# A fused spectral-mix and GEGLU backward kernel: feed-forward groups begin on eight transposed row tiles, and the transform of x is issued as pieces between the steps

## The chip, the cores and the metric

The kernel runs on one core of a Trainium2 chip. The metric is the device time of one execution in microseconds (us). The kernel before was run three times; the median is 1459.56 us.

A core has five engines with queues of their own, each strictly in the order of the program: TensorE (PE in the profile; PEld are its weight loads), VectorE (DVE), ScalarE (ACT), GpSimd (POOL) and SyncE (SP). SP issues nearly all transfers here; POOL and ACT issue a few.

## The reference, cut to what matters

The forward pass mixes two branches of x (2048 rows of 576, bf16) by a gate for each row, and the kernel returns the output and all seven gradients.

```python
def _A_ref(x, w_r, w_i):
    X = rfft2(x.astype(float32), axes=(-2, -1)) * (w_r + 1j * w_i)
    return irfft2(X, s=(S, D), axes=(-2, -1)).astype(bfloat16)

def _B_ref(x, w_gate, w_up, w_down):
    return (gelu_tanh(x @ w_gate) * (x @ w_up)) @ w_down      # 576 -> 4608 -> 576

g = sigmoid((x * gate_w).sum(-1, keepdims=True))
out = g * _A_ref(x, w_r, w_i) + (1 - g) * _B_ref(x, w_gate, w_up, w_down)
# and the vjp of out for grad_out: x, w_r, w_i, w_gate, w_up, w_down, gate_w
```

## The kernel before, in words

**Names.** Rows lie on 128 partitions as 16 row tiles (T = 16): `xn` holds x, `dB` grad_out ("dO"). Their transposes, which matmuls with the weights and with the tables need, are `xT` and `dOT`. The Fourier transforms are matmuls with cosine and sine tables that the kernel builds at its start: `build_D` (tables along the 576 columns, `Dt`), `build_R` (rotation angles along the rows, four row tiles a call, `Rt`), `columns_B` and `build_B` (`Btab`, for the last 32-point stage). Each ends in a Sin on ACT; those of R and B are put on a list, `tb.late`, and issued when `run_late` or a pop empties it.

**The head (L841 to L876).** SP loads x, grad_out and the gate and up weights of the first group, all rows first. `tchunk` (L335) transposes four row tiles on PE and copies them from PSUM, two copies on DVE and one on ACT. Between the four chunks of x and the four of grad_out stands the whole forward transform of x: for each row tile a first half `u1` (L546; six matmuls with `Dt`, then one copy on ACT to Y) and a second half `u2` (L561; two matmuls with `Rt`, a copy `ve` on ACT, an add and a subtract on DVE to Vt at L574 and L575, a store to DRAM). The down-projection weights of group 0 come in two steps: `load_w(0, 1)` are two transposing loads, `load_w(0, 2)` five copies into `wdT`; `load_w(0, 0)` are six loads into `wgu`. Last stands `gate()` (L355): 80 one-column matmuls, a Sigmoid on ACT and four small operations on DVE, which give `omg32` (1 - g) and `gs32` to all that follows. The head takes its PSUM from three pools in turn (`headps`, L330): pg (one buffer), ph (two) and pz (one).

**The steps (L935 to L1006).** The 4608 hidden columns are 18 groups of 256, and each group has four steps of four row tiles. A step is: `H_mm` (L370), the products z = dOT with wdT (L380, L383) and xy = xT with wgu (L387, L394) in two halves; `H_da` (L401), ACT scales z into da; `H_act` (L407), ACT takes q, xb and hu from each half of xy; `H_ew1` (L416), three operations on DVE; `H_ew2` (L432), two Sigmoids on ACT (om and s, L435 and L436) and eight operations on DVE (L440 to L447), which give A, dHg and dHu. From group 1 on a step also issues pieces of the weight gradients of the group before (`W_units`, L460; matmuls at L480, L497 and L510, copies on ACT at L458), each with a weight in microseconds (1.0 or 1.7).

**The slots.** The other transforms are a list of pieces, `fft` (L882): the forward transform of grad_out (`fg`, 16 first and 16 second halves), the turned tables, the middle (`mid_units`: products with the filter, 74 slots, with their DVE work on a list of its own, `side`) and the two inverse transforms. `fft_next` issues the next piece. How many pieces have to be issued by the end of a step, `want` says (L901): four a step in group 0, then by a weighted share up to step 65. In a step from group 1 on the first piece stands in the middle of the second half of xy, the others among the weight-gradient pieces where the weights passed so far reach 1.0, 3.0 and 5.0 (L982), and what is left over at the step's end. A piece takes its PSUM from `pftile` (L533): in group 0 from pg and pz in turn, later, when pg has been given up, only from pz, which z uses too. `scale_dB` (L930) multiplies half of dB by omg32 on DVE, after step 3 and after step 4.

**The end.** After the steps, from about 1024 us, PE computes b and the gradient of x from A, dHg and dHu, which are loaded back from DRAM (`block`, L1089).

The functions that the change touches, and what calls them:

Of the kernel before, what the change touches and what calls it, by code (L numbers as in the profile page):

```python
# [30 lines left out]
FG = 256  # L31
# [195 lines left out]
def kernel(  # L227
# [40 lines left out]
    def load_w(g, part):  # L268

        fsl = slice(g * FG, (g + 1) * FG)  # L270
        if part == 0:
            wts[g] = (wpool.tile([P, 5, 2 * FG], BF16, tag="wgu", name="wgu"), wpool.tile([P, 5, FG], BF16, tag="wdT", name="wdT"))
# [28 lines left out]
    for k in range(4):  # L301
        load_x(4 * k)
    for k in range(4):
        load_do(4 * k)
    load_w(0, 0)
# [29 lines left out]
    def tchunk(src, dst, t0, copy=None):  # L335
        for k, cs in enumerate(((0, 1), (2, 3), (4,))):
            pool, tag = headps()
            tp_ = pool.tile([P, 2, 2, 4, P], BF16, tag=tag, name="tp")
            for j, c in enumerate(cs):
                for tt in range(4):  # L340
                    if c < 4:
                        nc.tensor.transpose(tp_[:, 0, j, tt, :], src[:, t0 + tt, eo(c)], ident[:])
                    else:
                        for r in (LO, HI):
                            nc.tensor.transpose(tp_[r, 0, 0, tt, :], src[:, t0 + tt, 512:D], ident[:])
            o = dst[:, cs[0]:cs[0] + len(cs), t0:t0 + 4, :]
            i = tp_[:, 0, 0:len(cs)]
            if copy:
                copy(o, i)
            elif k == (t0 // 4) % 2:  # L350
                nc.scalar.copy(o, i)
            else:
                V.tensor_copy(o, i)

    def gate():  # L355
        lps = head_tile()[:, 0]
        for t in range(T):
# [3 lines left out]
        nc.scalar.activation(g_bf[:], lps[:, 0:T], ACT.Sigmoid)  # L361
        V.tensor_copy(g32[:], g_bf[:])
        V.tensor_scalar(omg_bf[:], g32[:], -1.0, 1.0, op0=ALU.mult, op1=ALU.add)
        V.tensor_copy(omg32[:], omg_bf[:])
        V.tensor_scalar(gs32[:], g32[:], SD2, None, op0=ALU.mult)
# [177 lines left out]
    def fwd_units(src, dst, scale, ps=pftile, vevac=None):  # L543
# [17 lines left out]
        def u2(t):  # L561
            def f():
# [278 lines left out]
    def head_tile():  # L841
        pool, tag = headps()
        return pool.tile([P, 2, 512], F32, tag=tag, name="fx")
# [6 lines left out]
    with nc.allow_non_contiguous_dma(reason="tiny gate_w column load"):  # L850
        for par in range(2):
            nc.gpsimd.dma_start(gwT[:, 2 * par:2 * par + 2], gate_w[par:512:2].rearrange("(k p) -> p k", p=P))
        nc.gpsimd.dma_start(gwT[HI, 4:5], gate_w[512:D].rearrange("(p o) -> p o", o=1))
    x1, x2 = fwd_units(xT, scr_x, None, ps=head_tile)
    build_R(nc, tb, unit, 0)
    run_late(tb)
    for t in range(T):
        x1[t]()
        if t in (6, 11):
            load_w(0, 1 + t // 11)  # L860
        if t % 4 == 2 and t < 14:
            tchunk(xn, xT, t + 2)
        if t >= 9 and t % 2 == 1:
            tchunk(dB, dOT, 2 * (t - 9))
        if t % 4 == 1 and t + 3 < T:
            build_R(nc, tb, unit, t + 3)
        if t == 13:
            build_B(nc, tb, unit, res)
        if tb.late:
            tb.late.pop(0)()  # L870
        if t > 1:
            x2[t - 2]()
    run_late(tb)
    x2[T - 2]()
    x2[T - 1]()
    gate()  # L876

    fg = zipped(*fwd_units(dOT, scr_g, gs32))
# [17 lines left out]
    mid_at = 2 * T + 10  # L896
    NPR = NT // 2
    LASTP = NG * NPR - 7
    done = [0]

    def want(pr):  # L901

        n0 = 4 * NPR
        if pr < NPR:
            return 4 * (pr + 1)

        def load(n):

            return n + 0.7 * min(max(n - mid_at, 0), n_mid)
# [25 lines left out]
    for g in range(NG):  # L935
# [3 lines left out]
        for m in range(NPR):  # L939
# [9 lines left out]
            if g == 0 and m > 0:  # L949
                fft_next()  # L950
# [6 lines left out]
            if g == 0:  # L957
                fft_next()
            if pr == 0:
                fft_next()  # L960
# [3 lines left out]
            def second():  # L964
                xy = xy_full(1, fft_next if n or g == 0 else None)
# [3 lines left out]
                side_work(1.4)  # L969

            def sigs():
                H_ew2(g, m, tiles, state[0], da)
                side_work(1.4)
            if g == 0:
                second()
                fft_next()
# [270 lines left out]
```

## Time and profile before

| | us |
|---|---|
| three runs | 1459.56, 1457.01, 1460.73 |
| median | 1459.56 |
| the profiled execution, its own time | 1458.92 |
| its span in the profile | 1457.1 |
| first z matmul (L380), step 0 | 49.84 |
| first z of steps 1, 2 and 3 | 60.10, 72.71, 84.37 |
| first z of step 4 (group 1) and step 5 | 96.03, 110.67 |
| first matmul of the last stage (L1092) | 1023.84 |

The mean granted clock of TensorE is 0.992 of full speed over the span. A row of a profile view names the line, the engine, the operation and the tiles, out <- in; idle time ahead of it stands in brackets with what released it.

### The profile page before, as it was taken

The numbers are of one execution on the slowest core, as the hardware profiler recorded it, in microseconds if no ns is written. First come the engines' busy times: TensorE is split into PE (matmuls) and PEld (weight loads), VectorE is DVE, ScalarE is ACT, GpSimd is POOL, SyncE is SP. The second block draws the span as 40 slices with busy tenths as digits, with TensorE's granted clock in tenths as the row PEclk, the third lists the DMA queues.
The fourth block names the chain that finished last, engine by engine and source line by source line (L and its number), as shares of the span: only waits on it lengthen the run. The fifth ranks groups of instructions, "written<-read, shape, count | busy, mean of one in ns | idle before, by whom it ended". The sixth has DMA issues, their size and how long they took to land.

```text
span 1457.1 us, 28112 instructions
## 1 busy us (share of the span) xinstructions
PE 1386.9 (95%) x11342; PEld 1023.7 (70%) x11414; DVE 731.4 (50%) x1394; ACT 715.5 (49%) x1311; POOL 125.6 (9%) x230
## 2 busy tenths in 40 slices
PE   6888998999999999999999999999999999999997
PEld 4555666676676676677767667668777777777776
DVE  6676456876866776755666565553000652212200
ACT  5776767776677777667766767663000000000000
POOL 3001010000010011001001001000000110000000
PEclk9999999999999999999999999999999999999999
DMA  5333363445645554453554554857999997887773
GB/s 190 94 103 105 92 167 108 135 123 142 166 122 134 146 155 117 113 160 105 151 145 122 144 161 121 182 130 175 242 179 188 234 220 158 170 159 156 163 151 76
DMA packets 516477, 214.96 MB, mean 148 GB/s; under 512 B 312921, under 2 KB 510554, under 8 KB 516346
## 3 DMA queue, kind: packets, MB, share of 16 engines
q1 hardware_dynamic: 506714, 192.65, 56.8%
q0 software_dynamic: 7824, 19.49, 4.3%
q8 instruction: 89, 1.46, 0.4%
q10 hardware_dynamic: 1808, 1.02, 0.2%
q14 instruction: 42, 0.34, 0.1%
HBM read 40.76 MB, written 93.84 MB: 92 GB/s over the span
## 4 chain that ended last, share of the span: by engine, by line
PE 82%; ACT 9%; DVE 3%; issue 3%; SPq 1%; DMA 1%; POOL 0%; ACTq 0%; DVEq 0%; POOLq 0%
PE acc L1092 28%; PE wps L497 16%; PE xy L394 14%; PE z L380 8%; PE wps L480 7%; PE xy L387 2%; PE wps L510 2%; PE z L383 1%; ACT om L435 1%; ACT xb L413 1%; ACT hu L414 1%; ACT q L411 1%; DMA pin<-scr 1%; ACT Xx L666 1%; ACT s L436 1%
## 5 line engine op out<-in xcount | busy, mean ns | idle before, releaser
L1092 PEld LDWEIGHTS <-pin 128*128 128x128 bf16 x3456 | 337.3, 98 | 87.5 <-DMA pin<-scr 1.8
L394 PE MATMUL xy<-wgu,xT 128*128 128x512 bf16 x1080 | 258.8, 380 | 10.1 <-issue 9.4
L497 PEld LDWEIGHTS <-xn 128*128 128x128 bf16 x2304 | 224.4, 98 | 38.2 <-issue 0.2
L394 PEld LDWEIGHTS <-xT 128*128 128x128 bf16 x1152 | 106.5, 98 | 138.2 <-issue 32.3
L404 ACT ACTIVATE da<-z,omg 128x256 bf16<-128x256 f32 x288 | 112.8, 474 | 118.7 <-PE z L383 118.7
L480 PE MATMUL wps<-dB,A 128*128 128x288 bf16 x1152 | 153.8, 288 | 10.7 <-ACT dwd L458 10.7
L1109 ACT COPY bo<-acc 128x288 f32<-128x288 f32 x32 | 12.7, 398 | 306.4 <-PE acc L1092 281.8
L380 PE MATMUL z<-wdT,dOT 128*128 128x256 bf16 x1152 | 139.8, 275 | 14.7 <-ACT Y L558 4.2
L480 PEld LDWEIGHTS <-A 128*128 128x128 bf16 x1152 | 112.8, 98 | 45.0 <-issue 13.4
L1092 PE MATMUL acc<-wuT,pin 128*128 128x288 bf16 x1152 | 143.6, 286 | 0.2 <-DMA pin<-scr 0.2
L1092 PE MATMUL acc<-wgT,pin 128*128 128x288 bf16 x1152 | 143.8, 286 | 0.0
L1092 PE MATMUL acc<-wd_all,pin 128*128 128x288 bf16 x1152 | 142.9, 286 | 0.7 <-DMA pin<-scr 0.5
L380 PEld LDWEIGHTS <-dOT 128*128 128x128 bf16 x1152 | 112.4, 99 | 34.7 <-issue 19.8
L497 PE MATMUL wps<-dHg,xn 128*128 128x256 bf16 x1152 | 135.8, 273 | 0.0
L497 PE MATMUL wps<-dHu,xn 128*128 128x256 bf16 x1152 | 133.8, 273 | 0.0
L411 ACT ACTIVATE q<-xy 128x512 bf16<-128x512 f32 x144 | 86.9, 604 | 56.6 <-PE xy L394 54.8
L419 DVE TENSOR_SCALAR s<-q 128x1024 bf16<-128x1024 bf16 x72 | 30.6, 425 | 159.1 <-ACT q L411 159.1
L440 DVE TENSOR_TENSOR xb<-xb,s 128x1024 bf16<-128x1024 bf16 x72 | 49.8, 692 | 108.4 <-ACT s L436 108.4
L503 POOL DMA_DIRECT2D out_dram<-dw x67 | 48.8, 728 | 633.2 <-ACT dw L458 528.1
L1169 DVE SCALAR_TENSOR_TENSOR f32t<-gwf,dlog,b16t 128x576 f32<-128x576 f32 x16 | 13.1, 817 | 170.4 <-DMA b16t<-dxa_scr 170.4
L414 ACT CAST hu<-xy 128x512 bf16<-128x512 f32 x144 | 88.3, 614 | 0.0
L413 ACT CAST xb<-xy 128x512 bf16<-128x512 f32 x144 | 84.8, 589 | 0.0
(197 smaller groups left out, 1593.5 us busy)
## 6 DMA issues: line engine op xcount, KB each, us to landing
scr<-A SPq DMA_DIRECT2D x72, 256.0 KB, 2.5
scr<-dHg SPq DMA_DIRECT2D x72, 256.0 KB, 2.8
scr<-dHu SPq DMA_DIRECT2D x72, 256.0 KB, 3.3
out_dram<-dw POOLq DMA_DIRECT2D x67, 128.0 KB, 2.2
wd_all<-in_B_w_down_dram SPq DMA_DIRECT2D x3, 1728.0 KB, 14.5
out_dram<-dwd POOLq DMA_DIRECT2D x34, 144.0 KB, 3.2
scr_p<-Vt SPq DMA_DIRECT2D x32, 145.0 KB, 3.6
wgu<-in_B_w_gate_dram SPq DMA_DIRECT2D x18, 256.0 KB, 3.5
```

The source lines that it names most:

```text
L380: nc.tensor.matmul(zo(t), lhsT=dOT[:, ci, t, :], rhs=wdT[:, ci, :], start=(t % 4 < 2 and ci == 0), stop=False)
L394: nc.tensor.matmul(xy[k][:, t % 2, :], lhsT=xT[:, ci, t, :], rhs=wgu[:, ci, :], start=False, stop=(ci == 3))
L404: nc.scalar.activation(da[:, t, :], z[:, t % 2, t // 2, :], ACT.Copy, scale=omg32[:, 4 * m + t:4 * m + t + 1])
L411: nc.scalar.activation(q[:, h, :], xy[:, :, 0:FG], ACT.Square)
L413: nc.scalar.copy(xb[:, h, :], xy[:, :, 0:FG])
L414: nc.scalar.copy(hu[:, h, :], xy[:, :, FG:2 * FG])
L419: V.tensor_scalar(s[:], q[:], A_GELU, 1.0, op0=ALU.mult, op1=ALU.add)
L440: V.tensor_tensor(xb[:], xb[:], s[:], op=ALU.mult)
L480: nc.tensor.matmul(wps[:, :288], lhsT=tl(0, t)[:, fch * P:(fch + 1) * P], rhs=dB[:, t, h * 288:(h + 1) * 288], start=(t == 0), stop=(t == ...
L497: nc.tensor.matmul(wps[:, cc, :], lhsT=xn[:, t, (c0 + cc) * P:(c0 + cc + 1) * P], rhs=tl(k, t), start=(t == 0), stop=(t == T - 1))
L503: wst[0].dma_start(ov[:, c0:c0 + TPB, fsl], dw[:])
L1092: nc.tensor.matmul(acc[:, :288], lhsT=src[:, r, :], rhs=w_of(r)[:, h * 288:(h + 1) * 288], start=(first and r == 0), stop=(last and r == F ...
```

## The change

It does six things.

1. **Loads.** SP's order is now: x rows 0 to 3, the transposing loads of the down weights, grad_out rows 0 to 3, gate and up weights, x and grad_out rows 4 to 7, the copies into wdT, then the other two chunks of both. gate_w is loaded from ACT's queue instead of POOL's.
2. **The head** transposes only row tiles 0 to 7 of x and of grad_out. The gate is computed for four row tiles at a time. There is no forward transform of x in it.
3. **Steps 0 and 1** transpose the third and the fourth chunk of x and grad_out, with the gate of that chunk, between `H_ew1` and `H_ew2`.
4. **The forward transform of x** goes to the front of the list of pieces, so that 32 more stand in it. Its Vt tiles come from the pool `half` (two buffers) instead of `unit`. In group 0 there are 1, 2, 4 and 4 pieces a step. `want` gives the pieces of the middle the weight 1.5 instead of 1.7, a step can take up to six, and `side_work` goes on to 1.9 us instead of 1.4.
5. **Angles.** `build_R` multiplies and adds on POOL, two operations on 128x512 in float for each four tiles; DVE converts to integers and takes the AND when the Sin is issued.
6. **Late tables.** The Sins of rotation tables 8 to 15, `build_B` and its Sin stand at the top of step 4, ahead of its matmuls.

```diff
 def build_R(nc, tb, unit, t0):
-    V = nc.vector
+    V, G = nc.vector, nc.gpsimd
...
+    Xf = unit([n, P], F32, name="XRf")
     X = unit([n, P], I32, name="XR")
-    krow, kadd = tb.kk[:, 0, :], tb.kk[:, 1, :]
-    for t in range(n):
-        V.scalar_tensor_tensor(X[:, t, :], krow, tb.scol[:, t0 + t:t0 + t + 1], kadd, op0=ALU.mult, op1=ALU.add)
-    V.tensor_single_scalar(X[:], X[:], S - 1, op=ALU.bitwise_and)
+    krow, kadd = (tb.kk[:, v, :].unsqueeze(1).to_broadcast([P, n, P]) for v in range(2))
+    G.tensor_tensor(Xf[:], krow, tb.scol[:, t0:t0 + n].unsqueeze(2).to_broadcast([P, n, P]), op=ALU.mult)
+    G.tensor_tensor(Xf[:], Xf[:], kadd, op=ALU.add)
...
-    tb.late.append(lambda: nc.scalar.activation(o, X[:], ACT.Sin, bias=tb.pi[:], scale=-step))
+
+    def sine():
+        V.tensor_copy(X[:], Xf[:])
+        V.tensor_single_scalar(X[:], X[:], S - 1, op=ALU.bitwise_and)
+        nc.scalar.activation(o, X[:], ACT.Sin, bias=tb.pi[:], scale=-step)
+    tb.late.append(sine)
...
-    for k in range(4):
+    with nc.allow_non_contiguous_dma(reason="tiny gate_w column load"):
+        for par in range(2):
+            nc.scalar.dma_start(gwT[:, 2 * par:2 * par + 2], gate_w[par:512:2].rearrange("(k p) -> p k", p=P))
+        nc.scalar.dma_start(gwT[HI, 4:5], gate_w[512:D].rearrange("(p o) -> p o", o=1))
+    load_x(0)
+    load_w(0, 1)
+    load_do(0)
+    load_w(0, 0)
+    load_x(4)
+    load_do(4)
+    load_w(0, 2)
+    for k in (2, 3):
         load_x(4 * k)
-    for k in range(4):
         load_do(4 * k)
-    load_w(0, 0)
...
-    def fwd_units(src, dst, scale, ps=pftile, vevac=None):
+    def fwd_units(src, dst, scale, ps=pftile):
...
-                Vt = (unit if src is xT else half)([2, DF], name="Vt")
+                Vt = half([2, DF], name="Vt")
                 ve = unit([2, 2, HF], F32, name="ve")
-                n0 = 1 if src is xT or on_pg() else 0
+                n0 = 1 if on_pg() else 0
...
+    VC, AC = V.tensor_copy, nc.scalar.copy
     build_D(nc, tb, unit, res, 0, 2)
+    for f in titems(xn, xT, 0, head_tile, (VC, VC, VC)):
+        f()
     build_D(nc, tb, unit, res, 2, 2)
-    tchunk(xn, xT, 0, V.tensor_copy)
+    build_R(nc, tb, unit, 0)
+    build_R(nc, tb, unit, 4)
     build_D(nc, tb, unit, res, 4, 1)
+    for f in titems(dB, dOT, 0, head_tile, (AC, VC, AC)):
+        f()
+    run_late(tb)
+    gate(0, head_tile)
+    for f in titems(xn, xT, 4, head_tile, (VC, AC, VC)) + titems(dB, dOT, 4, head_tile, (VC, AC, VC)):
+        f()
+    gate(1, head_tile)
+    build_R(nc, tb, unit, 8)
+    build_R(nc, tb, unit, 12)
     columns_B(nc, tb, res)
...
-    fg = zipped(*fwd_units(dOT, scr_g, gs32))
+    fg = zipped(*fwd_units(xT, scr_x, None)) + zipped(*fwd_units(dOT, scr_g, gs32))
...
-    mid_at = 2 * T + 10
+    mid_at = 4 * T + 10
...
+    FIRST = (1, 3, 7, 11)
...
-        n0 = 4 * NPR
+        n0 = FIRST[-1]
         if pr < NPR:
-            return 4 * (pr + 1)
+            return FIRST[pr]
...
-            return n + 0.7 * min(max(n - mid_at, 0), n_mid)
+            return n + 0.5 * min(max(n - mid_at, 0), n_mid)
...
-            if g == 0 and m > 0:
-                fft_next()
+            if pr == NPR:
+                run_late(tb)
+                build_B(nc, tb, unit, res)
+                run_late(tb)
...
             if g == 0:
                 second()
-                fft_next()
+                if m < 2:
+                    t0 = 4 * m + 8
+                    for f in titems(xn, xT, t0, pftile, (VC, VC, AC)):
+                        f()
+                    gate(m + 2, pftile)
+                    for f in titems(dB, dOT, t0, pftile, (VC, VC, AC)):
+                        f()
+                else:
+                    fft_next()
                 sigs()
+                for _ in range(n - 1 - m // 2):
+                    fft_next()
             else:
                 second()
                 at, k, late = 0.0, min(n, 1), [sigs]
                 for w, f in carry + hs:
-                    if k < n and at >= (0.0, 1.0, 3.0, 5.0)[k]:
+                    if k < n and at >= (0.0, 1.0, 3.0, 5.0, 5.0, 5.0)[k]:
```

`titems` is `tchunk` as a list of three items, each of which transposes two column chunks (the last one) of four row tiles into a PSUM tile of the pool it is given and copies them out with the engine named for it (VC is a copy on DVE, AC one on ACT). `gate(k, ps)` is `gate()` for row tiles 4k to 4k+3: 20 one-column matmuls, one Sigmoid, the same four operations on DVE.

More of the change, by code (lines that the diff above doesn't have):

```diff
@@ L270, in load_w @@
         fsl = slice(g * FG, (g + 1) * FG)
+        if g not in wts:
+            wts[g] = (wpool.tile([P, 5, 2 * FG], BF16, tag="wgu", name="wgu"), wpool.tile([P, 5, FG], BF16, tag="wdT", name="wdT"))
         if part == 0:
-            wts[g] = (wpool.tile([P, 5, 2 * FG], BF16, tag="wgu", name="wgu"), wpool.tile([P, 5, FG], BF16, tag="wdT", name="wdT"))
             wgu = wts[g][0]
@@ L333, in headps, with titems, item, f @@
         return pool, tag
[L335 to L357, printed above, removed]
+    def titems(src, dst, t0, ps, copies):
+        def item(k, cs):
+            def f():
+                tp_ = ps(BF16).rearrange("p b (j t m) -> p b j t m", j=2, t=4)
+                for j, c in enumerate(cs):
+                    for tt in range(4):
+                        if c < 4:
+                            nc.tensor.transpose(tp_[:, 0, j, tt, :], src[:, t0 + tt, eo(c)], ident[:])
+                        else:
+                            for r in (LO, HI):
+                                nc.tensor.transpose(tp_[r, 0, 0, tt, :], src[:, t0 + tt, 512:D], ident[:])
+                copies[k](dst[:, cs[0]:cs[0] + len(cs), t0:t0 + 4, :], tp_[:, 0, 0:len(cs)])
+            return f
+        return [item(k, cs) for k, cs in enumerate(((0, 1), (2, 3), (4,)))]
+    def gate(k, ps):
+        lps = ps()[:, 0]
+        ts = slice(4 * k, 4 * k + 4)
+        for t in range(4 * k, 4 * k + 4):
             for ci in range(5):
@@ L360, in gate @@
                                  start=(ci == 0), stop=(ci == 4))
[L361 to L365, printed above, removed]
+        nc.scalar.activation(g_bf[:, ts], lps[:, ts], ACT.Sigmoid)
+        V.tensor_copy(g32[:, ts], g_bf[:, ts])
+        V.tensor_scalar(omg_bf[:, ts], g32[:, ts], -1.0, 1.0, op0=ALU.mult, op1=ALU.add)
+        V.tensor_copy(omg32[:, ts], omg_bf[:, ts])
+        V.tensor_scalar(gs32[:, ts], g32[:, ts], SD2, None, op0=ALU.mult)
     kept = {}
@@ L839, in inv_units, with head_tile @@
         return out + [d(T - 2), d(T - 1)], [pre(0), pre(2)]
-    def head_tile():
+    def head_tile(dt=F32):
         pool, tag = headps()
-        return pool.tile([P, 2, 512], F32, tag=tag, name="fx")
+        return pool.tile([P, 2, 512 if dt is F32 else 1024], dt, tag=tag, name="fx")
+    VC, AC = V.tensor_copy, nc.scalar.copy
     build_D(nc, tb, unit, res, 0, 2)
+    for f in titems(xn, xT, 0, head_tile, (VC, VC, VC)):
+        f()
     build_D(nc, tb, unit, res, 2, 2)
-    tchunk(xn, xT, 0, V.tensor_copy)
+    build_R(nc, tb, unit, 0)
+    build_R(nc, tb, unit, 4)
     build_D(nc, tb, unit, res, 4, 1)
-    columns_B(nc, tb, res)
[L850 to L876, printed above, removed]
-    fg = zipped(*fwd_units(dOT, scr_g, gs32))
+    for f in titems(dB, dOT, 0, head_tile, (AC, VC, AC)):
[7 more added lines that the diff above has]
+    build_R(nc, tb, unit, 12)
+    columns_B(nc, tb, res)
+    fg = zipped(*fwd_units(xT, scr_x, None)) + zipped(*fwd_units(dOT, scr_g, gs32))
     ia, pa = inv_units(scr_p1, a_dv, SD2)
@@ L956 @@
             flush()
-            if g == 0:
-                fft_next()
-            if pr == 0:
-                fft_next()
             H_act(0, xy, tiles, 1)
@@ L964, in second @@
             def second():
-                xy = xy_full(1, fft_next if n or g == 0 else None)
+                xy = xy_full(1, fft_next if n else None)
                 for part in range(2):
@@ L968, in second @@
                 state.append(H_ew1(tiles))
-                side_work(1.4)
+                side_work(1.9)
             def sigs():
                 H_ew2(g, m, tiles, state[0], da)
-                side_work(1.4)
+                side_work(1.9)
             if g == 0:
                 second()
-                fft_next()
+                if m < 2:
[5 more added lines that the diff above has]
+                        f()
+                else:
+                    fft_next()
                 sigs()
+                for _ in range(n - 1 - m // 2):
+                    fft_next()
             else:
```

## The prediction

> **What bounds the kernel now.** I read the page first (busy time, slices), then busy time by stretches of my choice, then TensorE's waits, then the timeline and the chain of waits of the first hundred microseconds.
>
> ```profile
> PE 1386.9 (95%) x11342; PEld 1023.7 (70%) x11414; DVE 731.4 (50%) x1394; ACT 715.5 (49%) x1311; POOL 125.6 (9%) x230
> ...
> PE   6888998999999999999999999999999999999997
> ...
> PEclk9999999999999999999999999999999999999999
> ```
>
> TensorE (PE) is the bound nearly everywhere; only the first slices are thin. I cut at the first score matmul (z, 49.84 us), at the start of the second group (96.03), and on through the steps:
>
> ```profile
> 0.00:49.84 49.84, 34.57 (x400) 25.31 (x401) 35.58 (x109) 29.57 (x53) 12.91 (x46) 0.97 0.48 162
> 49.84:96.03 46.19, 36.54 (x231) 20.86 (x233) 27.68 (x55) 33.55 (x64) 0.00 (x0) 0.93 0.36 103
> 96.03:110.67 14.64, 12.77 (x113) 9.11 (x114) 10.52 (x23) 11.02 (x19) 0.30 (x1) 1.00 0.28 86
> ...
> 200.00:620.00 420.00, 402.85 (x3188) 284.92 (x3219) 296.09 (x547) 307.19 (x557) 40.71 (x64) 1.00 0.49 133
> 620.00:985.00 365.00, 354.81 (x2984) 257.75 (x3010) 211.58 (x369) 251.40 (x458) 35.30 (x56) 1.00 0.54 142
> ```
>
> After each length stand PE, weight loads, DVE, ACT, POOL. The head costs 49.8 us and group 0 46.2; from there PE is short of the clock by a few per cent. TensorE's waits from 111 us to the end of the steps add up to 34.3 us, of which 9.0 is "issue"; 25.3 us are waits for ACT. The largest kind between 200 and 620:
>
> ```profile
> PE wps L480 <- ACT dwd L458: 7.9, 7, 1.3
> PE xy L394 <- issue: 4.1, 26, 0.2
> ```
>
> So work moved from the head into the steps is paid on PE unless it falls into those 25 us. Group 0 has no weight-gradient work, and its steps are a loop through ACT and DVE. The chain of waits shows one turn (84.37 to 96.03 is one step):
>
> ```profile
> 83.67 0.64 ACT Y L558
> 84.31 0.95 ACT om L435
> 85.29 1.06 ACT s L436
> ...
> 90.33 0.61 DVE hu L446
> ...
> 91.58 0.45 DVE Vt L574
> 92.03 0.38 DVE Vt L575
> 92.45 0.42 PE pf L568 x2
> 92.87 0.88 PE xy L394 x4
> ```
>
> **What the Trainium skill says.** "TensorE: Matmul & The Clock Gate", Part 1: after about 3.4 us of idleness TensorE runs at half its clock, until it has been busy that long again. The trace agrees in group 0: granted clock 0.93, and a 512-column matmul of 0.63 us after a 2 us wait, against 0.38 normally. "ScalarE: Activation LUTs", "What ACT_TABLE_LOAD costs": 1283 ns for each change of function set, and a drain; the load of before agrees (1.28), the drain doesn't show (the next instruction starts 0.27 us after the load). "GPSIMD Engine Reference", 3.1: some 2.6 cycles at 1.2 GHz for each element of a two-input operation; no such wide operation is in this trace.
>
> ```profile
> 48.47 1.28 ACT L361 ACT_TABLE_LOAD   x1
> ...
> 69.78 0.63 PE L394 MATMUL xy<-wgu,xT 128*128 128x512 bf16 x1
> ...
> 98.30 1.57 ACT L404 ACTIVATE da<-z,omg 128x256 bf16<-128x256 f32 x4 [0.29 <-PE z L383]
> ...
> 103.23 2.31 DVE L932 TENSOR_SCALAR dB<-dB,omg 128x576 bf16<-128x576 bf16 x8
> ```
>
> **The change, part by part.**
>
> (1) The head. Gone from it: 32 transform pieces of x, half of the transposes, the mask tables and two of four angle tables. What is late next? Loads: x rows land at 4.7 us as now. SP then issues two transposing loads (1.2 + 1.3), dO rows (0.5), six gate/up loads (3.9), x and dO rows (0.9), five copies into wdT (3.4), so the last is issued near 13 and lands near 15 to 16 (2.1 to landing): hidden. POOL: after 5.2 us four two-input operations on 512 elements; the skill's price gives 1.1 us plus about 0.2, the nearest row (tensor_scalar, 290 elements, 0.51) gives 0.8. I take 1.3, so the last cosine table's inputs come at 11.2 instead of 6. DVE waits there in program order for ACT's sine, to about 13, with the dO copies, the casts and ANDs of two angle tables (0.43 each as L150; the cast is not in the trace, 0.2 to 0.6) behind it: 15.4. Two sines (0.72), table load (1.28), gate sigmoid: 17.6. Then six copies of the second row tiles (0.68 and 1.03 as L353, L351) on DVE and ACT, second gate: 20.3. The first z shares its PSUM buffer with that gate and starts at **20.5** (cheap POOL and warm PE: 18; ACT's three gate_w issues at 0.85 each as on POOL, cold PE: 23). Against 49.84: **-29.3** (-27 to -32).
>
> (2) Group 0. Steps 0 and 1: z and xy take 5.85 us of PE; with one slot (0.75) the last xy ends 7.0 after the step's start, q is there at 7.65, the three DVE operations of the gelu end at 9.2. Only then do DVE's copies of the transposes run, behind them in its queue: 0.65, 0.65, then ACT 0.6 after a PE turn of 0.5; gate matmuls 0.55, sigmoid 0.2, four small DVE operations 0.7; two more copies 1.3, PE 0.45, ACT 0.6. Next z waits for that last buffer: 14.6 us a step. ACT's om and s stand behind it, but they lie beside the next z. Steps 2 and 3 keep the loop above, ending in Y behind om and s: 12.0 each (before: 11.66). Sum 53.4; the idle stretches bring some cold clock, of which each 3.4 us costs 1.7; I take 4 us for the four steps (2 to 7). 57.4 against 46.2: **+11.2** (+6 to +14).
>
> (3) Step 4. The other two angle tables and the mask table now stand at its top, ahead of da on ACT. Their casts on DVE stand behind ew2 of step 3 (to 4.1 us after z), its Vt (0.9) and the scaling of dB (2.3, the row above): 7.3. Casts and ANDs 1.7, mask arithmetic 1.9 (41.5 to 43.4 in the timeline of before), so the last sine ends at 11.5 and da, 1.57 long, at 13.1. PE reaches the slot in the second xy at 5.0 us; from group 1 on a slot has only the z buffer, which da empties. PE stands there 8.1 us, all its queue with it, and comes back at half clock for 3.4 us (1.7 lost). **+9.8** (+6 to +12). Two table loads (2.6) on ACT lie inside the wait or beside matmuls; uncovered they would be part of the range.
>
> (4) The slots moved. Until step 4 the kernel of before has done 16 of 32 pieces, the new one 11 of 64: 37 more must go into the steps, 19 first halves (six matmuls, 0.75) and 18 second halves (two, 0.25), 14.1 + 4.5 = **+18.5** of PE. Each also costs ACT 0.65 and, in the second halves, DVE 0.9; both have a quarter of the stretch free. Their stores add 32 issues of 0.35 on SP, whose next weights have a group's time.
>
> (5) Denser slots. By the weights of want there are now 3.8 slots a step (before 3.5) outside the middle, 2.55 (2.03) in it. A fourth slot in a step has its due weight at 5.0; two steps of four don't reach it before their last piece, so it goes to the end of the step and the next z waits for its copy, about 1 us (rows of 0.8 to 1.9 are in the waits now). 16 steps more with it at half: +8. Against it, slots ahead of a wait for ACT use that wait: I give it 5 of the 25 us. **+3** (-16 to +12).
>
> (6) At nothing: half tiles for Vt instead of unit tiles (stores land in 2 us), side work 1.9 instead of 1.4 (the same DVE operations; in the middle they have a shorter period), gate_w on ACT's queue. The last seven steps and all after them are unchanged.
>
> Sum: -29.3 + 11.2 + 9.8 + 18.5 + 3 = **+13.2**. The profiled execution took 1458.9 us (span 1457.1), 0.6 below the median of 1459.56; 1458.9 + 13.2 = **1472**.
>
> **Rivals.** *Not slower: the steps swallow the pieces.* Place: the waits for ACT between 111 and 985. Without term 5 the sum is +10.2; it is no longer slower from 5.8 us swallowed, and faster from 14.6 of the 25.3. For it: every slot ahead of an L480 wait costs nothing. Against: these waits are short (1.3 at most) and the pieces bunch in steps 5 to 20. With 16 swallowed: 1453. *DVE becomes the bound in the middle.* Its 7.0 us a step of gelu and 11.3 us of products for eight slots give 10.6 of 12.4 us, and om waits on ACT for DVE: 0.5 us in each of 29 steps would add 14.5: 1487. Against it: three quarters busy now without such waits. *The head isn't shortened as said*: the transposed weights come late because SP is held up by full queues (waits of 0.9 us on loads are there now) and z starts at 28: 1480.
>
> **How the numbers follow.** A change under 0.3% (4.4 us) can't be told from none here. Forecast 0.55 (1463 to 1481), swallowed 0.26, DVE 0.11, late weights 0.08. Faster takes 0.18 of the second; within 0.13 (0.08 of the second, 0.05 at the forecast's lower edge); slower the rest, 0.69. The range 1452 to 1488 leaves out some 0.1 below and 0.08 above.
>
> **What would show it.** First z near 20.5; second group near 78; in step 4 a wait of about 8 us of PE at L551 for ACT's da, and ACT waiting for DVE ahead of the sines; z of step 5 near 102; then steps of 14 to 15 us to step 20. Wrong if step 4 has no such wait, if group 0 takes under 50 us, or if the waits of PE after step 5 sum to well under 34 us.

## The result, and the profile after

The changed kernel takes 1495.19 us (median of four runs, 1492.86 to 1499.63), the kernel before 1458.81 in the same comparison: a ratio of 1.0253, 95% interval 1.0225 to 1.0281. It is slower by 36.4 us, where I had forecast 12.4 over the median of before, and it lies above my range of 1452 to 1488. The profiled execution has a span of 1492.4 us against 1457.1. Lines are now those of the changed kernel, some 12 higher in the steps.

The page of the changed kernel, the same three lines as of before:

```profile
PE 1408.4 (94%) x11414; PEld 1033.0 (69%) x11414; DVE 736.9 (49%) x1393; ACT 723.3 (48%) x1317; POOL 132.6 (9%) x235
...
PE   5779999999998998899999999999999999999997
...
PEclk9889999999999999999999999999999999999999
```

They hide the loss: PE is still busy for 94%. Three slices between 448 and 634 us (37.3 each) have fallen from 9 to 8, and the head is shorter and thinner. (The trace of before lacks 72 of the 1152 matmul records of xy, one in each step. So its busy time and the waits it calls "issue" can't be set against this page. The trace of e9 below lacks 72 as well, one in each step, and can be set against it; that of e12, which runs the matmuls of before, lacks none.) So I cut at the first z of steps 0, 4, 5 and 71, in the changed kernel:

```profile
0.00:24.10 24.10, 11.39 (x136) 9.47 (x137) 15.97 (x38) 10.00 (x17) 15.22 (x31) 1.00 0.85 254
24.10:83.17 59.07, 45.92 (x342) 27.41 (x342) 32.36 (x74) 34.59 (x65) 4.39 (x20) 0.88 0.24 68
83.17:107.40 24.23, 17.07 (x119) 11.01 (x118) 14.69 (x39) 13.70 (x23) 0.29 (x1) 0.79 0.21 64
107.40:1020.15 912.75, 869.22 (x6990) 613.46 (x6990) 573.64 (x1043) 639.09 (x1157) 83.56 (x132) 0.99 0.49 132
```

and the last stretch in the kernel before:

```profile
110.67:983.50 872.83, 837.92 (x6778) 597.59 (x6844) 557.50 (x1007) 615.48 (x1120) 83.33 (x132) 0.99 0.50 135
```

Against before: head -25.7, group 0 +12.9, step 4 +9.6, steps 5 to 71 +39.9, what follows -1.3; the sum is the spans' difference, 35.3. Three of the four parts lie near the forecast, though the head is just outside its range of -27 to -32. The steps after step 4 don't: I had 18.5 + 3 for them.

Where in them? I took the start of each step's z in both traces and subtracted (us, after minus before):

| step | 0 | 4 | 5 | 10 | 20 | 30 | 31 | 37 | 43 | 56 | 71 |
|---|---|---|---|---|---|---|---|---|---|---|---|
| offset | -25.7 | -12.9 | -3.3 | -4.1 | +8.0 | +9.7 | +9.7 | +19.2 | +33.2 | +34.6 | +36.7 |

From 5 to 20, where x's pieces are, it climbs by 11.3. Then comes a second climb, 23.5 us from step 31 to step 43, the second half of the middle. TensorE's waits from the start of step 30, whose offset is that of step 31, to the start of step 43 (457.16 to 645.66) are these; columns: waiting engine and line, what for, total, times, longest:

```profile
PE z L392 <- ACT Vt L765: 7.5, 3, 4.4
PE wps L492 <- ACT dwd L470: 5.7, 3, 2.7
PE pf L673 <- DMA wdT<-wtmp: 3.0, 1, 3.0
PE z L392 <- ACT Xg L678: 1.9, 2, 1.7
```

In the kernel before, from 420 to 630, PE has none of these waits for Vt. Its longest kind there is:

```profile
PE wps L480 <- ACT dwd L458: 4.5, 4, 1.3
```

In the changed kernel PE waits for ACT's copy Vt, and ACT in turn waits for a store (same stretch, then the kernel before from 420 to 630):

```profile
ACT Vt L765 <- DMA scr_p<-Vt: 15.8, 4, 5.6
```

```profile
ACT Vt L753 <- DMA scr_p<-Vt: 1.3, 1, 1.3
```

ACT can't write Vt because the pool `half` has two buffers and the store of an earlier Vt to scr_p hasn't landed. Why is the store late? The chain of waits of the changed kernel around the longest of these, from 602 to 616 us:

```profile
601.80 0.70 DVE dHg L459
602.51 0.37 SPq L463
...
603.53 0.51 SPq L638
...
604.09 0.72 SPq L638
...
604.86 0.59 SPq L664
605.50 0.42 SPq L664
...
611.15 0.42 SPq L664
...
611.67 2.98 DMA scr_p<-Vt
614.73 0.82 ACT Vt L765
615.59 3.33 PE z L392 x16
```

SP first waits for DVE's dHg, whose store (L463) is ahead in its queue, then issues the prefetch of the pair after next: two loads of Vp and twelve small loads of Wt, 603.5 to 611.6 (only the first rows of them are shown). Only then comes the store of Vt, which a blocked ACT waits for, with PE behind it for 4.4 us. Sixteen z matmuls then take 3.33 us instead of 1.91, at a granted clock of 0.54.

### The profile page after: what moved, and what is told of

It reads as the page before. It is cut to its first block, busy times and chain, and to the rows that moved or that the text cites. A ratio compares the mean times of both kernels' runs of the same rounds, so it can differ in the third digit from the quotient of the medians.

```text
span 1492.4 us, 28124 instructions
## 1 busy us (share of the span) xinstructions
PE 1408.4 (94%) x11414; PEld 1033.0 (69%) x11414; DVE 736.9 (49%) x1393; ACT 723.3 (48%) x1317; POOL 132.6 (9%) x235
## 4 chain that ended last, share of the span: by engine, by line
PE 77%; ACT 10%; DVE 5%; SPq 3%; issue 2%; DMA 2%; POOL 0%; ACTq 0%; DVEq 0%; POOLq 0%
PE acc L1099 28%; PE xy L406 14%; PE wps L509 12%; PE z L392 8%; PE wps L492 6%; PE xy L399 2%; ACT om L447 2%; PE pf L563 2%; PE z L395 1%; PE wps L522 1%; ACT q L423 1%; ACT xb L425 1%; ACT Xx L678 1%; ACT hu L426 1%; SPq L742 1%
## 5 line engine op out<-in xcount | busy, mean ns | idle before, releaser
L406 PE MATMUL xy<-wgu,xT 128*128 128x512 bf16 x1152 | 271.7, 381 | 0.0
L392 PE MATMUL z<-wdT,dOT 128*128 128x256 bf16 x1152 | 147.6, 285 | 28.9 <-ACT Vt L765 9.0
L392 PEld LDWEIGHTS <-dOT 128*128 128x128 bf16 x1152 | 117.0, 102 | 53.1 <-issue 35.3
L1176 DVE SCALAR_TENSOR_TENSOR f32t<-gwf,dlog,b16t 128x576 f32<-128x576 f32 x16 | 13.1, 817 | 172.9 <-DMA b16t<-dxa_scr 172.9
## 6 DMA issues: line engine op xcount, KB each, us to landing
wd_all<-in_B_w_down_dram SPq DMA_DIRECT2D x3, 1728.0 KB, 14.6
```

What stands on the lines that cost most here:

```text
L392: nc.tensor.matmul(zo(t), lhsT=dOT[:, ci, t, :], rhs=wdT[:, ci, :], start=(t % 4 < 2 and ci == 0), stop=False)
L406: nc.tensor.matmul(xy[k][:, t % 2, :], lhsT=xT[:, ci, t, :], rhs=wgu[:, ci, :], start=False, stop=(ci == 3))
```

## The experiments

**Theory S**: SP's strict queue is what the denser middle runs into. **Rivals**: D, DVE's work is late (its products, or A and dHg ahead of the stores); P, SP is late only because others are; and for the head, C against Q, as their expectations say. Beside each time I give the loss, (ratio - 1) times 1459, since the median of the kernel before differed from 1458 to 1463 between the groups of runs: the change itself loses 36.9 (32.8 to 41.0).

**e1: the middle's Vt from another pool** (in `s1`, L764).

```
-                Vt = half([2, 2 * HF], name="Vt")
+                Vt = unit([2, 2 * HF], name="Vt")
```

> The changed kernel with the middle's Vt tiles (L764, the copies ahead of the scr_p stores) taken from the 18 unit buffers instead of the two half buffers. Theory S (ACT's Vt copy waits for a half buffer, whose store stands behind other issues on SP): the waits of ACT at L765 for scr_p go, and of the 24 us that steps 29 to 42 lose against the kernel before, 15 to 22 come back: 1471 to 1480. Theory D (DVE is late in the denser middle, and SP, ACT and PE wait for it in the end): no more than 4 us, 1490 to 1496. A unit shortage would show as new waits and could eat part of it.

1483.78 us, ratio 1.0168 (1.0142 to 1.0194): loss 24.5. ACT's wait for scr_p is gone from the list, and the climb from step 31 to 43 falls from 23.5 to 13.9. A third of the loss goes, 12.4 us, less than the 15 to 22 that S expected. A wait on the copies into wdT (2.4 us) takes part of its place: these too are issued by SP.

**e2: side work back to 1.4.**

```
-                side_work(1.9)
+                side_work(1.4)
```

(in both places)

> The changed kernel with side work up to 1.4 us a call, as before, instead of 1.9. Theory D: DVE gets to its gelu operations earlier, 8 to 15 us come back, 1478 to 1487. Theory S: nothing is gained, and products that are late may cost a little: 1490 to 1500.

1510.53 us, 1.0359 (1.0335 to 1.0382): loss 52.4, 15 worse. TensorE's waits over the whole of this run begin with a new one:

```profile
PE pf L762 <- DVE qn L732: 18.9, 8, 7.3
```

With less side work in each call the products of the middle come too late for their pieces, first at step 27. So the longer side work is not what makes the loss; taking it back costs more. Theory D falls in the form in which the added DVE work is the culprit.

**e3: the late tables after the second half of step 4.**

```
-            if pr == NPR:
-                run_late(tb)
-                build_B(nc, tb, unit, res)
-                run_late(tb)
...
                 second()
+                if pr == NPR:
+                    run_late(tb)
+                    build_B(nc, tb, unit, res)
+                    run_late(tb)
```

> The changed kernel with the late tables of step 4 (two angle tables, the mask table and their sines) issued after the second half of xy and the gelu's first operations instead of at the top of the step. Both theories: da no longer waits for the sines, so step 4 shortens from 24.2 us to 16 to 18 and the total by 5 to 8 us: 1487 to 1490. If the wait merely moves to a later copy, step 4 stays above 21.

1490.17 us, 1.0222 (1.0194 to 1.0249): loss 32.4; its interval overlaps the change's. Its trace shows what it did: step 4 takes 19.95 us instead of 24.23, where I had expected 16 to 18. In the changed kernel ACT has the table load and then waits, with da behind the sines, and PE waits for da (timeline rows of ACT and PE; the idle time before each is in brackets):

```profile
91.70 1.52 ACT L158 ACTIVATE Rt<-XR,pi 128x512 bf16<-128x512 int32 x2 [6.98 <-DVE XR L157]
```

```profile
96.40 1.61 PE L563 MATMUL pf<-Dt,xT 128*128 128x290 bf16 x6 [6.25 <-ACT da L416]
```

In e3 da stands ahead of them, at 84.01, and what is left is a piece that waits for ve on ACT, behind the sines:

```profile
84.01 1.57 ACT L416 ACTIVATE da<-z,omg 128x256 bf16<-128x256 f32 x4 [3.64 <-PE z L395]
```

```profile
95.58 0.91 PE L563 MATMUL pf<-Dt,xT 128*128 128x290 bf16 x6 [3.14 <-ACT ve L584]
```

So 4.3 of step 4's 9.6 us are the place of da in ACT's queue, and part of what is left is the same sines, ahead of ve. (The trace as a whole ends 9.1 us earlier than the change's. Of that, 2.7 us lie in group 0, where the two run the same code, so they are scatter and not the edit.)

**e4: the store ahead of the prefetch.**

```
-                if key == "m1" and b == 1 and p + 2 < T // 2:
-                    prefetch(p + 2)
...
                 LD.dma_start(dst[g:g + 2].rearrange("g q l -> q g l"), Vt[:])
+                if key == "m1" and b == 1 and p + 2 < T // 2:
+                    prefetch(p + 2)
```

> The changed kernel with the scr_p store of the second m piece (L767) issued before the prefetch of the pair after next (L755, 14 issues of some 0.5 us on SP) instead of after it. Theory S: the store lands 8 us sooner, most of the waits at L765 go, 10 to 20 us come back: 1473 to 1485. Theory D: nothing, 1490 to 1496.

1487.19 us, 1.0187 (1.0155 to 1.0219): loss 27.3. Nothing is taken off SP, only the store moves ahead of the fourteen issues of the prefetch, and some 10 us go, just short of the 10 to 20 that S expected; the climb from 31 to 43 is 16.5. Beside the waits for dwd that the kernel before has too, PE now waits there for:

```profile
PE z L392 <- DMA wdT<-wtmp: 4.1, 2, 2.7
```

The weights' copies are the next thing late on SP.

**e5: the angles on DVE again** (`build_R` of before, four fused operations a block on DVE; the rest of the change as it is).

> Changed kernel with one part undone: the rotation angles (build_R) are formed on DVE again, in four fused operations per block of four, as in the kernel before, so GpSimd has nothing but the DMA issues in the head. Theory C (GpSimd's two-operand operations stretch the DVE operations beside them: the D tables' operations took 2.36 us for a pair instead of 0.77, the others two to three times their length): the D-table operations go back to under 0.9 us for a pair although DVE gets about 8 more operations, and the first z product, at 24.1 us now, comes between 20.5 and 23; the whole 1491 to 1494. Theory Q (it is the queue of the head: gate_w, which lands 5.5 us after its issue, and the loads of x): the first z stays at 24.1 or comes later, by the DVE work that came back, up to 26.

1495.71 us, 1.0223 (1.0206 to 1.0241): loss 32.5, not to be told from the change's. In the traces, the D tables' operations on DVE in the changed kernel:

```profile
5.41 2.36 DVE L125 SCALAR_TENSOR_TENSOR XD<-lrow,dcol,yD 128x145 f32<-128x145 f32 x2
7.80 1.18 DVE L128 SCALAR_TENSOR_TENSOR yD<-XD 128x290 f32<-128x290 f32 x1
```

and in e5, with nothing of the angles on GpSimd:

```profile
5.41 0.77 DVE L125 SCALAR_TENSOR_TENSOR XD<-lrow,dcol,yD 128x145 f32<-128x145 f32 x2
6.21 0.46 DVE L128 SCALAR_TENSOR_TENSOR yD<-XD 128x290 f32<-128x290 f32 x1
```

The lengthening that theory C names is shown: the same operations take 2.6 to 3.1 times as long while GpSimd runs these, from the changed kernel:

```profile
5.17 1.09 POOL L149 TENSOR_TENSOR XRf<-kk,scol 128x512 f32<-128x512 f32 x1
6.34 1.26 POOL L150 TENSOR_TENSOR XRf<-XRf,kk 128x512 f32<-128x512 f32 x1
```

In the same trace the next pair on DVE, at 10.43, stands beside one-operand operations of GpSimd and takes 0.68. But the first z comes at 23.20, only 0.9 earlier, just outside what C expected: PE's gate matmuls wait for gate_w, until 16.87 in e5 and 16.44 in the changed kernel:

```profile
16.44 0.77 PE L371 MATMUL fx<-gwT,xT 128*128 128x1 bf16 x18 [3.05 <-DMA gwT<-in_gate_w_dram]
```

**e6: gate_w on GpSimd's queue, as before** (three `nc.scalar.dma_start` to `nc.gpsimd.dma_start`).

> Changed kernel with the three small loads of gate_w's columns issued by GpSimd's queue again and not by ScalarE's. Theory Q: PE's 4.1 us wait for gwT goes and the first z comes 2 to 4 us earlier, at 20 to 22 us. Theory C: GpSimd stands in its angle operations and the loads start no sooner, or the wait goes and the stretched DVE operations are what is late next: the first z stays within 1 us of 24.1. The whole 1491 to 1496 either way.

1502.21 us, 1.0262 (1.0232 to 1.0291): loss 38.2, not to be told from the change's. The wait for gwT is gone, and the first z is later, at 25.75, which neither theory said. ACT's first cosine, which in the changed kernel stands behind the three issues until 11.65, starts at 6.83. But on GpSimd the issues end at 5.98, so the angle and table operations behind them are later, DVE waits 1.9 us for one of them, and ACT's sines end at 20.5, not 18.8:

```profile
22.01 1.01 PE L358 MATMUL fx<-ident,dB 128*128 128x128 bf16 x8 [3.96 <-ACT g_bf L373]
```

The head has two chains of nearly the same length, gate_w on ACT's queue and the angles over GpSimd and DVE. e5 shortens the second and e6 takes away the first at the second's cost. No run shortens both, so how they share the lateness of the first z is not shown.

**e7: out_dw's stores on GpSimd's queue** (`LD.dma_start(d, sb)` to `ST.dma_start(d, sb)` in `out_dw`).

> Changed kernel with out_dw's twelve stores of each pair of the middle issued by GpSimd's queue and not by SP's; nothing else is changed. Theory S (SP's queue is what bounds the denser middle: the small stores and the weight copies stand behind 14 issues of the prefetch and 12 of out_dw): 12 of the some 35 issues that SP has per pair go, about 5.7 us of SP per pair over 8 pairs; the scr_p stores and the weight copies come earlier, PE's waits for Vt and wdT fall from 13 to under 5 us, and the whole goes to 1473 to 1483. Theory P (PE waits for ACT's queue and for the products of DVE, and SP is only late because they are): within 3 us of 1495. GpSimd's queue holds the weight gradients' stores, which wait for ACT's copies; if out_dw's stores hold them up, PE's wait for wps grows.

1489.8 us, 1.0177 (1.016 to 1.0194): loss 25.8. The time is outside both ranges, in its own group of runs; by the ratio 11 us are gone, just short of S's 12 to 22. The offset rises by only 1.9 from step 31 to 37 (the change: 9.5), but by 11.8 from there to 43 (the change: 14.0), and the wait of the chain above is still there, 4.5 us, behind the prefetch. PE's waits for Vt there add up to 6.2 us, where S had those for Vt and wdT together under 5; none for wdT is left.

**e8: the planner's weight back to 0.7** (`return n + 0.7 * min(max(...))` in `want`).

> Changed kernel with the weight that the planner gives a slot of the middle put back from 0.5 to 0.7, the kernel before's number: the slots of x's and the gradient's transform come denser, those of the middle later and less dense (by about a quarter of a slot per step). Theory S and any theory in which the middle's density makes the loss: the loss between steps 31 and 43, 24 us now, falls to 10 to 16, a few us come back between steps 5 and 30, and the whole is 1482 to 1490. Theory N (the number of pieces and not their density makes the loss): within 3 us of 1495, with the loss moved to other steps.

1507.13 us, 1.0295 (1.0268 to 1.0323): loss 43.0. That is no better, against both theories, and probably worse, though its interval still touches the change's. The climb from step 30 to 43 did fall by half, 23.5 to 12.3. But before it there is a new one, from 12.9 at step 27 to 26.3 at step 30. The chain of waits there:

```profile
432.01 6.35 DMA Vp<-scr_g
438.37 0.31 SPq L664
...
440.64 2.65 DMA scr_p<-Vt
443.37 0.82 ACT Vt L765
444.23 3.57 PE z L392 x16
```

SP stands 6.4 us in the middle of a prefetch, until the load of Vp has landed, and the store behind it, ACT and PE stand with it; z waits 9.4 us. The semaphores in the traces say what SP stands for: its transfers use eight of them in turn, and an issue waits until the transfer eight places before it, with the same semaphore, has landed. Here that is the load of Vp. It is the same queue with a longer cork, and my range took density for the only cause. Why this load took 6.35 us I have not tried.

**e9: only the prefetch's Wt loads on GpSimd's queue** (`LD.dma_start(sb, d)` to `ST.dma_start(sb, d)` in `prefetch`).

> Changed kernel with the twelve loads of Wt in each prefetch of the middle issued by GpSimd's queue and not by SP's; the order of the code is kept. In the trace of the run with out_dw's stores on GpSimd the one long wait left (4.5 us, z behind Vt behind scr_p) stood behind exactly these twelve issues (594.0 to 600.8 us). Theory S (SP's issues delay scr_p's stores): this wait goes, the loss between steps 31 and 43 falls from 24 to 10 to 14, the whole is 1478 to 1486; twice what out_dw's stores were worth, since a prefetch stands directly ahead of the scr_p store. Theory P (the late thing is DVE's last product dHg, which the scr store ahead of them on SP waits for): the scr_p store is late by DVE as well, PE's wait stays over 3 us, the whole is 1489 to 1495. If GpSimd's queue, which holds the weight gradients' stores, brings Wt late, DVE waits for Wt and the time is over 1495.

1486.19 us, 1.0172 (1.0147 to 1.0196): loss 25.1. In its trace the climb from step 31 to 43 is 9.0 instead of 23.5, and the waits of ACT and PE in that stretch (459.55 to 633.57) are:

```profile
ACT Vt L765 <- DMA scr_p<-Vt: 2.9, 2, 1.9
```

```profile
PE wps L492 <- ACT dwd L470: 3.7, 3, 2.1
PE z L392 <- ACT Vt L765: 2.9, 3, 1.2
```

One line, no work less, no buffer more, the order of the code kept, and the time is 0.2 above S's range: S holds for this part of the loss. P falls: the store of dHg keeps its place on SP, and the wait that P kept over 3 us is 1.2 at most. The loads themselves come in time on GpSimd: no wait of DVE for Wt is in the trace.

**e10: e1, e4 and e7 together.**

> Changed kernel with three edits of the runs before together: out_dw's stores on GpSimd's queue, the middle's Vt in the pool of 18 buffers and not in the pool of two, and the scr_p store ahead of the prefetch. Alone they were worth 5.4, 11.7 and 8.3 us. Theory S: they remove the same waits in part, so less than the sum of 25: 1472 to 1478, and what is left of the loss between steps 31 and 43 is 8 to 12 us, of which the denser pieces' own PE work is some 6 to 7. Theory M (each edit removes a wait that another one replaces): 1480 to 1486, no better than the best of them alone.

1485.74 us, 1.0164 (1.014 to 1.0188): loss 23.9. No better than e1 or e9 alone, the number that theory M gave. The trace speaks for S's mechanism all the same: the climb from step 31 to 43 is 7.9, ACT's wait for scr_p is gone, and no new wait has come. From step 5 to step 71 it takes 897.2 us, against 903.2, 905.8 and 903.0 with e1, e4 or e7 alone and 912.75 in the change. So the three remove in part the same waits, as S had it. This profile lost 3.0 us in group 0, where its code is the change's; whether the timed runs lost the same there is not known.

**e11: e10 with e3 and e5.**

> The three edits of the run beside it, and with them the late tables after the step's second half (alone worth 5 us in the timed runs, 10 in its trace) and the angles on DVE (worth 1 us in its trace). What is left of the change is then the head, group 0 with its transposes, and the moved pieces. Theory S: 1461 to 1470, still not below the kernel before, since 37 more pieces at some 0.5 us of PE (18.5 us), group 0's 13 us and the head's 26 us back add up to 5 us more, and some 5 us of waits in the middle stay. Theory M: 1472 to 1480.

1471.28 us, 1.007 (1.0048 to 1.0092): loss 10.2. Just above S's range, by 1.3. It is the fastest of the changed kernels, and still slower than the kernel before.

**e12: e9's edit in the kernel before.**

> The kernel before, with the twelve loads of Wt in each prefetch issued by GpSimd's queue: the same edit that took 9 us (timed) and 13 us (trace) off the changed kernel. Theory S (SP's queue is late only because the pieces of the middle come denser, so that an s1 piece finds the pool of two still held): with the kernel before's density nothing waits for long (ACT waited 4.0 us in two places for scr_p's stores in all, PE not once for Vt), so the edit is worth 0 to 2 us: 1457 to 1461. Theory U (the prefetch on SP costs every kernel of this shape some 10 us, whatever the density, and the change only happened to show it): 1446 to 1453, a version that beats both.

1460.18 us, 13 runs, against 1461.5, 17 runs: 0.9989 (0.9979 to 0.9998), a gain of 1.6 us (0.3 to 3.1). So the same edit is worth 11.8 in the changed kernel (by the losses) and 1.6 here: the prefetch on SP costs hardly anything by itself, and theory U falls. (My expectation was wrong in one detail. In the kernel before PE does wait for Vt once, 2.2 us at L661.) As an improvement it is too small to tell from nothing by the bound of the prediction.

That the denser pieces are the other half of the cause is argued, not shown. Counted in the traces, the middle has 33 pieces in steps 30 to 42 (23 in the kernel before), and there the loss is. But it has 24 in the ten steps before them (20 in the kernel before), nearly as dense, and there the offset rises by 1.7 only. Nor does the mean load of SP's queue tell: its issues take 61% of the time in steps 30 to 42 of the changed kernel, and 64% in steps 20 to 29 of the kernel before, where ACT waited for scr_p once, 2.7 us. One rival is left. In the kernel before the eight pieces of a pair take just four steps, so their prefetch falls on the same place in every group of weights (steps 20, 24, 28, 32 and 36); in the changed kernel it wanders (22, 24, 27, 31, 34, 36, 40). No run separates density from place.

## Why the prediction was wrong

Most of the signs that I named came: a wait of PE for da in step 4 (6.25 us, 8 forecast), ACT waiting there for DVE ahead of the sines (6.98 us), steps of 14.4 us up to step 20 (14 to 15 forecast). The first z (24.1 against 20.5), the second group (83.2 against 78) and step 5 (107.4 against 102) were late. PE's waits from step 5 to step 71 are 43.0 us, against 25.3 before. (The 34.3 that I gave holds 9.0 of "issue", which come from the missing records: e12, with all of them, has none.)

**Term 1, the head, -29.3: measured -25.7**, right in kind, mis-sized by 3.6. The first z came at 24.1, past even my cold end of 23. GpSimd's operations cost 1.09 and 1.26, so the estimate of about 1.1 us for 512 elements, from the 2.6 cycles of the Trainium skill ("GPSIMD Engine Reference", 3.1), and my 1.3 were good. The term lacked two things. DVE's own operations lengthen beside GpSimd's (e5), and I had costed them at their durations of before. And gate_w on ACT's queue, "at nothing" but for three issues in my late case, was issued only from 9.63 on, its last part landing 5.5 us after its issue, so that PE waited 4.1 us for it. The same page's section 1 ("Specifications") says in its table that GpSimd shares its SBUF interfaces with VectorE, and that DVE instructions with two SBUF inputs, as these are, contend for them; I had read it and given it no price.

**Term 2, group 0, +11.2: measured +12.9.** Steps 0 and 1 take 16.6 and 16.8, steps 2 and 3 12.6 and 13.1. The forecast for the four, 57.4, was 1.7 short. (14.6 + 14.6 + 12.0 + 12.0 is 53.2, not 53.4.) The granted clock was 0.88 against 0.93. It was 0.50 in three stretches, 13.7 us in all, in which PE worked 12.2 us; by an estimate from these some 6 us went to the clock, where I had put 4. The agreement is no closer than the scatter: the nine profiles with this same code in head and group 0 give +10.2 to +15.9.

**Term 3, step 4, +9.6 measured, +9.8 forecast**, and by the mechanism named: PE at L563 for da, 6.25 us, with the sines ahead of da. Da ends 13.2 us after the step's start (13.1 forecast). PE's wait is shorter than 8.1 because PE itself comes to it 2 us later: the step's z took 3.38 us instead of 1.91. e3 confirms the order as a cause. (z of step 5 came at 107.4, not 102, because the head and group 0 together were 5.3 longer.)

**Term 4, the moved pieces, +18.5: confirmed.** (At its own prices it is 18.75.) e9 has the changed kernel's work in the steps, lacks as many records as the trace of before, and has no wait over 2.1 us left:

```profile
108.73:1008.05 899.32, 856.11 (x6924) 611.68 (x6990) 573.70 (x1043) 639.23 (x1157) 132.88 (x228) 1.00 0.51 134
```

856.11 of PE's busy time against 837.92 before: 18.2 us. 146 more matmuls are in it, of the 150 that 37 pieces have. The rival in which the steps swallow the pieces falls with it: from step 5 to step 20 PE's work grew by 13.1 us (204.86 in e9 against 191.73 before) and the offset, in the changed kernel, by 11.3, so some 2 us were swallowed.

**Term 5, denser slots, +3: this is the step that failed.** The stretch is longer by 39.9, of which 18.2 are term 4: 21.7 are waits, and the clock after them. The trace of e12, with the matmuls of before and no record missing, has for it:

```profile
112.39:982.54 870.15, 845.18 (x6844) 597.95 (x6843) 557.52 (x1007) 615.37 (x1120) 132.28 (x228) 1.00 0.51 136
```

So PE is idle for 25.0 us there, and for 43.5 in the changed kernel. Even my upper end was 12. I had counted waits of PE for copies at the end of a step and reckoned that other waits would absorb some. I hadn't followed the copy's own buffer: Vt in `half` is free only when the store has landed, and the store stands in SP's queue. Under (6) I wrote of the half tiles that "stores land in 2 us", which is the time from issue to landing. The time from the copy to the issue was what mattered: 14 prefetch issues, some 8 us, behind a wait for dHg. And of SP I had asked only whether the weights come in time, under (4), not who else stands behind its issues. e9 takes 14.5 of the climb of 23.5 off by moving twelve issues; e12 shows that the same twelve cost hardly anything where the pieces stand as before. In e9 8.3 of the 21.7 are left (899.32 - 872.83 - 18.2), most of them between steps 30 and 43, where it climbs by 9.0 and PE works 3.6 us more than before.

**The rivals.** "DVE becomes the bound in the middle", 1487, had the right place and came nearest in size, by luck: DVE is 127.6 of 188.5 us busy there, and in e9 just as busy (127.8 of 174.0) without most of the loss. Late weights didn't delay the head, whose first z waited last for the gate. In the middle they were late behind the same queue, but only e1 and e4 show z waiting for them, 2.4 and 4.1 us. In the changed kernel a wait of 3.0 us at L673 ended as a copy into wdT landed, and the piece there doesn't read wdT.

**Where the expected gain went.** Of the head's 25.7 us group 0 takes back 12.9, step 4 9.6; the pieces, moved and not removed, cost 18.2, and the waits after step 4, with the clock after them, 21.7. Of these, moving twelve issues off SP takes away 13.4 in e9's trace; the rest is not all put down to a cause. With the queue relieved and step 4 mended (e11) the offset at step 71 is +11.5: -26.8 of head, +13.4 of group 0, +2.0 of step 4, +22.8 after it. A version that pays would have to get group 0 shorter; that wasn't tried.

**What stays open.** The 4.6 us by which e11's steps after step 4 exceed the pieces' 18.2. Whether it is the pieces' density or their place in the group that brings the prefetch and the stores together. Why gate_w's first issue on ACT's queue stands at 9.63, some 4.9 us after ACT's last work. And how much of e3's trace beyond step 4 would repeat: its timed gain has an interval as wide as itself.

## What to carry to other kernels

When pieces are put closer together, follow each one's buffer to the instruction that frees it, and from there into that instruction's queue: count all issues that stand ahead of it, and the wait at their head, not only the transfer's time to land. A queue that issues for half of the time (SP's for 457 of 913 us here) can hold two engines up for 4 us when a burst of prefetch stands ahead of a store. Here it paid to move the burst to another queue (e9) and to put the store ahead of it (e4).

## What the runs showed of the hardware that I had not expected

Beside 512-column two-operand operations on GpSimd (1.09 and 1.26 us) DVE's two-operand operations took 2.36 us for a pair of 145 columns and 1.18 for one of 290 columns, against 0.77 and 0.46 alone (e5).

A tiny load of 0.1 KB on ACT's queue landed 5.5 us after its issue, at a time when the DMA engines were 85% busy, against 2 to 3 us for the 128 to 256 KB stores in the steps. On GpSimd's queue in the same head (e6) the three gate_w loads took 4.9 to 5.4, and in the kernel before, issued at 16.6 to 18.3, 2.2.

After a wait of 4.4 us the sixteen z matmuls took 3.33 us instead of 1.91, which agrees with what the skill says of the clock ("TensorE: Matmul & The Clock Gate", Part 1). In group 0, where the prediction saw the same agreement, the traces don't show the 3.4 us of idleness that it gave as the condition. There PE's longest wait is 2.0 us in both kernels, and the granted clock still falls to 0.50 for 3.4 us at a time (68.41 to 71.81 in the kernel before, after a wait of 2.00 at 68.20), while no fall follows a wait of 2.1 us at 630.0 in the changed kernel. The measurement decides: here shorter waits were enough.
